# Normalising attention after the sums instead of before them, with the sums of a head pair kept together

## The chip, the cores and the metric

One core of one Trainium2 chip runs the whole kernel in one launch. Five engines work side by side, each through its own instructions in order: TensorE (PE), VectorE (DVE), ScalarE (ACT), GpSimd (POOL) and SyncE (SP), which starts the transfers. The metric is device time in microseconds (us).

## The reference

Attention over 4 batches, 12 heads, 448 positions and a head width of 64, with RMS-normalised queries and keys; then two dense blocks on the 1792x768 result, each 768 to 2048 and back.

```python
q_n, k_n = rmsnorm(q, g_q), rmsnorm(k, g_k)
scores = matmul(q_n, k_n.T) / sqrt(64)
attn = exp(scores - max(scores))
attn = attn / (sum(attn) + 1e-9)
x = matmul(attn, v)                        # then heads side by side: 1792 x 768
r = maximum(x @ w1_in, 0); x = (s * r * r + b) @ w1_out
h = x @ w2_in;             out = (h * cos(h)) @ w2_out
```

The four dense weights come in as float64 and are taken to float32 on the chip.

## The kernel before

**Attention** goes by pairs of heads, six pairs in each of four batches (24 in all). The 448 positions are four chunks of 112. A pair runs through these steps; names are those of the trace:

- `norms` (lines 115 to 146): squares of the raw queries and keys into a tile `sq` (ACT), their sums `ss` (DVE), the root by a logarithm and an exponential with a few tiny POOL instructions, then the normalised `nq` and two `nk` (POOL).
- `make_q`, `make_k`: PE turns `nq` and `nk` into PSUM tiles (`pt_q`, `pt_k`, ring `qa` of two banks); ACT and DVE split them in a high and a low part (`S`, `M0`, `M1`).
- `scores` (line 173), once per head j and chunk c, eight times a pair: two products into `sc` (PE), the negative maximum of each row (DVE, line 185), the exponential `pr` with its row sum (ACT, line 187). After each second chunk DVE adds 1e-9 to two row sums (line 191) and takes the reciprocals (line 192), and POOL multiplies the two `pr` tiles by them (line 195).
- `turn` (line 197), eight times a pair, six steps later: four PE transposes into `tp` (line 202), copied to `pT` by ACT (line 207), for the last chunk of a head by DVE (line 205). There are eleven `pT` buffers.
- `mix` (line 210), eight steps later: eight float32 products of `v` and `pT` into one bank `av`, head j=0 in its lower 64 partitions, j=1 in its upper (line 215). This text calls them the sums of a pair. Then `keep`: batches 0 and 1 are split at once into a high part `xh` (ACT) and a residue `xl` (DVE, line 92) and stay on the chip; batches 2 and 3 are copied by ACT (line 482) and written to DRAM, and come back later.

**The dense blocks** multiply with operands split in two parts, three single-pass products for one (`ph`, line 325, for the first layer of a block, `po`, lines 377 and 404, for the second). A float64 weight tile becomes float32 in `load_weight`: the transfer `raw` (two buffers), two ACT instructions (`c`, `t`), then three on DVE, the clamp of `c` (line 297), the merge of mantissa and exponent (line 300), the sign from `raw` (line 301).

**The order of the work.** The program is written as generators: attention of batch 0 alone, then the dense units of batch 0 with attention of batch 1 fed in between, and so on, by a table of debts. A planner that simulates the engines then sets the order on each engine among instructions whose inputs it takes to be there; so the eight sums of a pair need not follow each other. `follow(later, earlier)` adds a dependency by hand.

## Time and profile before

| | us |
|---|---|
| median of three runs (lowest, highest) | 1362.27 (1355.05, 1365.51) |
| the profiled execution, and its span | 1361.52, 1359.6 |
| busy: PE, DVE, ACT, POOL | 1286.0, 919.9, 819.9, 708.5 |

Matmul records carry modelled ends, so PE's busy time overlaps itself; the distance between two starts on PE says more. PE's clock was granted at 0.986 of its full speed on average. Attention's last product starts at 656 us.

### The profile page before, as it was taken

The numbers are of one execution on the slowest core, as the hardware profiler recorded it, in microseconds if no ns is written. First come the engines' busy times: TensorE is split into PE (matmuls) and PEld (weight loads), VectorE is DVE, ScalarE is ACT, GpSimd is POOL, SyncE is SP. The second block draws the span as 40 slices with busy tenths as digits, with TensorE's granted clock in tenths as the row PEclk, the third lists the DMA queues.
The fourth block names the chain that finished last, engine by engine and source line by source line (L and its number), as shares of the span: only waits on it lengthen the run. The fifth ranks groups of instructions, "written<-read, shape, count | busy, mean of one in ns | idle before, by whom it ended". The sixth has DMA issues, their size and how long they took to land.

```text
span 1359.6 us, 19381 instructions
## 1 busy us (share of the span) xinstructions
PE 1286.0 (95%) x6624; PEld 1078.5 (79%) x6624; DVE 919.9 (68%) x1641; ACT 819.9 (60%) x1826; POOL 708.5 (52%) x795
## 2 busy tenths in 40 slices
PE   4799988898999999999999999989999999999998
PEld 3455766666778787778799999879999999998997
DVE  7875999889776587554464456754566666666655
ACT  6876877777766467554334234678756666565641
POOL 5764976758666388453343232455535444453532
PEclk8899899999999999999999999999999999999999
DMA  4521435443333452111252123321111121211105
GB/s 128 156 60 41 126 118 167 123 142 103 107 103 108 129 163 64 37 44 49 84 153 79 47 76 94 93 82 47 47 47 47 47 71 49 69 40 55 47 13 162
DMA packets 84994, 116.08 MB, mean 85 GB/s; under 512 B 7584, under 2 KB 74912, under 8 KB 84896
## 3 DMA queue, kind: packets, MB, share of 16 engines
q1 hardware_dynamic: 84896, 114.85, 28.4%
q8 instruction: 52, 0.85, 0.3%
q14 instruction: 46, 0.38, 0.1%
HBM read 91.23 MB, written 23.59 MB: 84 GB/s over the span
## 4 chain that ended last, share of the span: by engine, by line
PE 57%; DVE 9%; DMA 7%; ACT 7%; issue 2%; POOL 1%; SPq 0%; DVEq 0%; ACTq 0%; POOLq 0%
PE ph L325 21%; PE po L377 13%; PE po L404 13%; PE av L215 4%; DMA raw<-in_moe_w_in_dram 4%; PE tp L202 3%; PE sc L178 3%; DMA raw<-in_moe_w_out_dram 2%; DVE gt L349 1%; DVE t L301 1%; DVE t L300 1%; DVE c L297 1%; ACT c L296 1%; DVE gt L350 1%; DMA xr<-xd 1%
## 5 line engine op out<-in xcount | busy, mean ns | idle before, releaser
L325 PE MATMUL ph<-xh,wh 128*128 128x448 f32 x768 | 281.7, 371 | 4.8 <-ACT hs L343 3.9
L325 PE MATMUL ph<-xl,wh 128*128 128x448 f32 x768 | 282.7, 370 | 0.8 <-POOL xl L92 0.7
L325 PE MATMUL ph<-xh,wl 128*128 128x448 f32 x768 | 283.0, 369 | 0.0
L355 POOL TENSOR_TENSOR gl<-gt,gh 128x448 fp32r<-128x448 f32 x128 | 155.1, 1217 | 142.3 <-ACT gh L354 142.3
L195 POOL TENSOR_SCALAR pr<-pr,r 112x448 f32<-112x448 f32 x192 | 137.3, 728 | 110.3 <-DVE r L192 68.6
L267 POOL TENSOR_TENSOR wl<-t,wh 128x384 fp32r<-128x384 f32 x144 | 154.8, 1089 | 53.0 <-ACT wh L266 50.4
L325 PEld LDWEIGHTS ph<-xh,wh 128*128 128x128 f32 x768 | 144.6, 188 | 21.4 <-ACT hs L343 4.4
L266 ACT CAST wh<-t 128x384 fp32r<-128x384 f32 x224 | 106.9, 511 | 84.4 <-PE po L377 42.6
L404 PE MATMUL po<-wh,gh 128*128 128x384 f32 x448 | 151.3, 339 | 6.1 <-DVE acc L412 5.7
L187 ACT ACTIVATE pr<-sc,small 112x448 f32<-112x448 f32 x192 | 122.1, 637 | 57.8 <-DVE small L185 56.2
L325 PEld LDWEIGHTS ph<-xl,wh 128*128 128x128 f32 x768 | 144.2, 188 | 15.3 <-POOL xl L92 1.5
L353 POOL TENSOR_TENSOR gt<-hs,gt 128x448 f32<-128x448 f32 x64 | 78.7, 1231 | 148.4 <-ACT gt L352 121.7
L325 PEld LDWEIGHTS ph<-xh,wl 128*128 128x128 f32 x768 | 144.8, 188 | 13.7 <-issue 2.8
L377 PE MATMUL po<-gh,wh 128*128 128x448 f32 x384 | 146.5, 384 | 8.7 <-DVE acc L386 7.2
L386 DVE TENSOR_TENSOR acc<-po,acc 128x448 f32<-128x448 f32 x168 | 103.1, 618 | 72.2 <-PE po L377 71.5
L404 PE MATMUL po<-wl,gh 128*128 128x384 f32 x448 | 149.4, 335 | 0.4 <-POOL wl L267 0.4
L404 PE MATMUL po<-wh,gl 128*128 128x384 f32 x448 | 149.8, 334 | 0.0
L377 PE MATMUL po<-gl,wh 128*128 128x448 f32 x384 | 142.6, 372 | 0.8 <-POOL gl L355 0.8
L377 PE MATMUL po<-gh,wl 128*128 128x448 f32 x384 | 143.1, 373 | 0.0
L185 DVE TENSOR_REDUCE small<-sc 112x1 f32<-112x448 f32 x192 | 116.7, 616 | 38.9 <-PE sc L178 37.7
L178 PE MATMUL sc<-M,S 128*112 128x448 f32 x384 | 121.9, 407 | 16.8 <-ACT pr L187 13.8
L412 DVE TENSOR_TENSOR acc<-po,acc 128x384 f32<-128x384 f32 x196 | 104.3, 550 | 43.8 <-PE po L404 43.6
(80 smaller groups left out, 2517.3 us busy)
## 6 DMA issues: line engine op xcount, KB each, us to landing
raw<-in_moe_w_in_dram SPq DMA_DIRECT2D x64, 384.0 KB, 3.5
raw<-in_moe_w_out_dram SPq DMA_DIRECT2D x64, 384.0 KB, 3.2
t<-wd SPq DMA_DIRECT2D x96, 192.0 KB, 2.4
wd<-t SPq DMA_DIRECT2D x64, 192.0 KB, 1.9
rawq<-in_q_dram SPq DMA_DIRECT2D x24, 224.0 KB, 2.8
rawk<-in_k_dram SPq DMA_DIRECT2D x24, 224.0 KB, 3.1
rawv<-in_v_dram SPq DMA_DIRECT2D x24, 224.0 KB, 3.3
xd<-xf SPq DMA_DIRECT2D x12, 224.0 KB, 2.1
```

The source lines that it names most:

```text
L178: mm = nc.tensor.matmul(sc, st[i]["S"][j][:, c * CP:(c + 1) * CP], st[i]["M"][j][n], start=(n == 0), stop=(n == 1))
L185: nc.vector.tensor_reduce(nm, sc, axis=AX.X, op=ALU.max, negate=True)
L187: nc.scalar.activation(pr, sc, AF.Exp, bias=nm, scale=1.0, accum_out=sm)
L195: nc.gpsimd.tensor_scalar(p, p, r[:, n:n + 1], 1.0, ALU.mult, ALU.mult)
L266: nc.scalar.copy(wh, w)
L267: eng.tensor_tensor(wl, w, wh.bitcast(F32), ALU.subtract)
L325: nc.tensor.matmul(h, a, m, start=(c == 0 and n == 0), stop=(c == NE - 1 and n == 2))
L355: nc.gpsimd.tensor_tensor(gl, gt, gh.bitcast(F32), ALU.subtract)
L377: marks["out"] = nc.tensor.matmul(po, a, m, start=(f == 0 and n == 0), stop=(f == CF - 1 and n == 2))
L386: nc.vector.tensor_tensor(at, po, at, ALU.add)
L404: nc.tensor.matmul(po, a, m, start=(f == 0 and n == 0), stop=(f == CF - 1 and n == 2))
L412: nc.vector.tensor_tensor(at, po, at, ALU.add)
```

## The change

- The probabilities stay unscaled: the two DVE instructions per two chunks and POOL's multiplication of each `pr` go. The eight row sums of a pair lie in one tile `sums`; after the eighth exponential POOL adds 1e-9, DVE takes eight reciprocals at once, and POOL spreads them over 64 columns each (`rb`).
- In `mix` PE transposes `rb` into a bank `rt` of the ring `qa`, ACT copies it to `x`, and after the eight sums DVE multiplies `av` by `x`. `x` lies in SBUF: batches 0 and 1 are split from there, the residue now on POOL, and batches 2 and 3 are written to DRAM from there without a further copy.
- The first product of each head in `mix` waits for the last four copies of turned tiles of the pair (`follow`).
- `pT` has ten buffers, and DVE copies three of the eight turned tiles of a pair instead of two.
- The squares of `norms` go into the tiles `nq` and the first `nk`, which the products overwrite later; `sq` is gone.
- In `load_weight` the sign is merged first, then the clamp, then mantissa and exponent.

```diff
         def norms(i):
...
-            for n, nm in enumerate("qk"):
-                sq = att.tile([CP, 8, D], F32, tag="sq", name=f"sq_{b}_{hp}_{n}", bufs=1)
-                nc.scalar.activation(sq.rearrange("p a d -> p (a d)"), st[i][nm].rearrange("p h c d -> p (h c d)"), AF.Square)
-                nc.vector.reduce_sum(ss[:, n, :], sq, axis=AX.X)
+            nq = att.tile([CP, NCH, 2, D], F32, tag="nq", name=f"nq_{b}_{hp}", bufs=1)
+            nks = [att.tile([CP, NCH, 2, D], F32, tag="nk", name=f"nk_{b}_{hp}_{j}") for j in range(2)]
+            for n, (nm, t) in enumerate((("q", nq), ("k", nks[0]))):
+                t = t.rearrange("p c h d -> p (c h d)")
+                nc.scalar.activation(t, st[i][nm].rearrange("p h c d -> p (h c d)"), AF.Square)
+                nc.vector.reduce_sum(ss[:, n, :], t.rearrange("p (a d) -> p a d", d=D), axis=AX.X)
...
         def scores(s):
...
-            if c % 2 == 0:
-                st[i]["sm"] = att.tile([CP, 4], F32, tag="small", name=f"small_{key}", bufs=3)
-            small = st[i]["sm"]
-            nm, sm = small[:, c % 2:c % 2 + 1], small[:, 2 + c % 2:3 + c % 2]
-            nc.vector.tensor_reduce(nm, sc, axis=AX.X, op=ALU.max, negate=True)
+            if s % 8 == 0:
+                st[i]["sums"] = att.tile([CP, NCH, 2], F32, tag="sums", name=f"sums_{key}", bufs=3)
+                st[i]["top"] = att.tile([CP, 8], F32, tag="top", name=f"top_{key}", bufs=3)
+            top, sums = st[i]["top"][:, s % 8:s % 8 + 1], st[i]["sums"]
+            nc.vector.tensor_reduce(top, sc, axis=AX.X, op=ALU.max, negate=True)
             pr = att.tile([CP, S], F32, tag="pr", name=f"pr_{key}", bufs=10)
-            nc.scalar.activation(pr, sc, AF.Exp, bias=nm, scale=1.0, accum_out=sm)
+            nc.scalar.activation(pr, sc, AF.Exp, bias=top, scale=1.0, accum_out=sums[:, c, j:j + 1])
             st[i]["pr", j, c] = pr
-            if c % 2:
-                r = att.tile([CP, 2], F32, tag="r", name=f"r_{key}", bufs=3)
-                nc.vector.tensor_scalar_add(r, small[:, 2:4], 1e-9)
-                nc.vector.reciprocal(r, r)
-                for n in range(2):
-                    p = st[i]["pr", j, c - 1 + n]
-                    nc.gpsimd.tensor_scalar(p, p, r[:, n:n + 1], 1.0, ALU.mult, ALU.mult)
+            if s % 8 == 7:
+                nc.gpsimd.tensor_scalar(sums, sums, 1e-9, 1.0, ALU.add, ALU.mult)
+                nc.vector.reciprocal(sums, sums)
+                rb = att.tile([CP, NCH, 2, D], F32, tag="rb", name=f"rb_{key}", bufs=1)
+                nc.gpsimd.tensor_copy(rb, sums.unsqueeze(3).to_broadcast([CP, NCH, 2, D]))
+                st[i]["rb"] = rb
...
         def turn(s):
...
-            t = att.tile([CP, S], F32, tag="pT", name=f"pT_{key}", bufs=11)
-            if kc == NCH - 1:
-                nc.vector.tensor_copy(t, tp)
+            t = att.tile([CP, S], F32, tag="pT", name=f"pT_{key}", bufs=10)
+            if kc + j >= NCH - 1:
+                done = nc.vector.tensor_copy(t, tp)
             else:
-                nc.scalar.copy(t, tp)
+                done = nc.scalar.copy(t, tp)
             st[i]["pT", j, kc] = t
+            st[i].setdefault("done", []).append(done)
...
         def mix(i):
             b, hp = pairs[i]
+            rt = ps.tile([P, 512], F32, tag="qa", name=f"rt_{b}_{hp}")[:, :S]
+            for c in range(NCH):
+                nc.tensor.transpose(rt[:, c * CP:(c + 1) * CP], st[i]["rb"][:, c, :, :].rearrange("p h d -> p (h d)"), ident[:CP, :CP])
+            x = att.tile([P, S], F32, tag="xf", name=f"xf_{b}_{hp}", bufs=1)
+            nc.scalar.copy(x, rt)
             pa = ps.tile([P, 512], F32, tag="qa", name=f"av_{b}_{hp}")[:, :S]
             for kc in range(NCH):
                 for j in range(2):
-                    nc.tensor.matmul(pa[j * D:(j + 1) * D, :], st[i]["v"][:, j, kc, :], st[i]["pT", j, kc], start=(kc == 0), stop=(kc == NCH - 1))
-            keep(b, hp, pa)
+                    mm = nc.tensor.matmul(pa[j * D:(j + 1) * D, :], st[i]["v"][:, j, kc, :], st[i]["pT", j, kc], start=(kc == 0), stop=(kc == NCH - 1))
+                    if kc == 0:
+                        for done in st[i]["done"][-4:]:
+                            follow(mm, done)
+            nc.vector.tensor_tensor(x, pa, x, ALU.mult)
+            keep(b, hp, x)
...
             nc.scalar.activation(cf, hi.bitcast(F32), AF.Copy, scale=2.0**-112)
-            nc.vector.tensor_scalar(cf, cf, VMAX, -VMAX, ALU.min, ALU.max)
             t = wp.tile([P, CW], U32, tag="t", name=f"t_{kk}", bufs=3)
             nc.scalar.activation(t, lo, AF.Copy, scale=LSCALE, bias=-0.5)
+            nc.vector.scalar_tensor_tensor(t, hi, 0x80000000, t, ALU.bitwise_and, ALU.bitwise_or)
+            nc.vector.tensor_scalar(cf, cf, VMAX, -VMAX, ALU.min, ALU.max)
             nc.vector.scalar_tensor_tensor(t, c, 3, t, ALU.logical_shift_left, ALU.bitwise_or)
-            nc.vector.scalar_tensor_tensor(t, hi, 0x80000000, t, ALU.bitwise_and, ALU.bitwise_or)
...
     def keep_on_chip(b, hp, x):
-        xs.setdefault((0, b), []).append(split(x, xa, f"1_{b}_{hp}", nc.vector))
+        xs.setdefault((0, b), []).append(split(x, xa, f"1_{b}_{hp}"))
...
     def keep_in_dram(b, hp, x):
         t = dram.tile([P, S], F32, tag=f"x_{b}_{hp}", name=f"xd_{b}_{hp}")
-        xf = pools["att"].tile([P, S], F32, tag="xf", name=f"xf_{b}_{hp}")
-        nc.scalar.copy(xf, x)
-        nc.sync.dma_start(t, xf)
+        nc.sync.dma_start(t, x)
```

What the planner makes of it is seen in the order of each engine's instructions; a name ends in batch, pair, head, chunk and a running number.

On PE, batch 1, pair 1, before: the second to fifth of the pair's sums (`av`), and the last tile turned for it (`tp`).

```order
L215 MATMUL av_1_1_2341<-pT_1_1_1_0_2162,rawv_1_1_1597 64x448
L215 MATMUL av_1_1_2341<-pT_1_1_0_1_1994,rawv_1_1_1597 64x448
L202 MATMUL tp_1_1_1_3_2242<-ident_73,pr_1_1_1_0_1882 112x112
L202 MATMUL tp_1_1_1_3_2242<-ident_73,pr_1_1_1_1_1910 112x112
L202 MATMUL tp_1_1_1_3_2242<-ident_73,pr_1_1_1_2_1969 112x112
L202 MATMUL tp_1_1_1_3_2242<-ident_73,pr_1_1_1_3_1982 112x112
L215 MATMUL av_1_1_2341<-pT_1_1_1_1_2197,rawv_1_1_1597 64x448
L215 MATMUL av_1_1_2341<-pT_1_1_0_2_2080,rawv_1_1_1597 64x448
```

The same pair in the changed kernel, from its first sum on:

```order
L387 MATMUL po_0_2_1_0_3068<-gl_0_4_0_2357,wh_0_0_1_2_0_2551 128x448
L221 MATMUL av_1_1_2220<-pT_1_1_0_0_1861,rawv_1_1_1517 64x448
L221 MATMUL av_1_1_2220<-pT_1_1_1_0_2049,rawv_1_1_1517 64x448
L221 MATMUL av_1_1_2220<-pT_1_1_0_1_1878,rawv_1_1_1517 64x448
L221 MATMUL av_1_1_2220<-pT_1_1_1_1_2079,rawv_1_1_1517 64x448
L221 MATMUL av_1_1_2220<-pT_1_1_0_2_1973,rawv_1_1_1517 64x448
L221 MATMUL av_1_1_2220<-pT_1_1_1_2_2092,rawv_1_1_1517 64x448
L221 MATMUL av_1_1_2220<-pT_1_1_0_3_2034,rawv_1_1_1517 64x448
L221 MATMUL av_1_1_2220<-pT_1_1_1_3_2123,rawv_1_1_1517 64x448
L179 MATMUL sc_1_2_1_2_2147<-M0_1_2_1_1795,S_1_2_1_1683 112x448
```

The eight products stand in a row, heads taking turns, between a dense unit and scores of the next pair. Before, four transposes stood between the third and the fourth, and the eight lay in five pieces.

On POOL, batch 0, before: scalings of the probabilities of pairs 1 and 2 and the tiny instructions of a root (`m`, `z`).

```order
L195 TENSOR_SCALAR pr_0_1_1_2_488<-pr_0_1_1_2_488,r_0_1_1_3_503 112x448
L195 TENSOR_SCALAR pr_0_1_1_3_501<-pr_0_1_1_3_501,r_0_1_1_3_503 112x448
L195 TENSOR_SCALAR pr_0_2_0_0_537<-pr_0_2_0_0_537,r_0_2_0_1_563 112x448
L195 TENSOR_SCALAR pr_0_2_0_1_561<-pr_0_2_0_1_561,r_0_2_0_1_563 112x448
L125 TENSOR_SCALAR m_1_0_1482<-ss_1_0_1475 112x16
L131 TENSOR_TENSOR z_1_0_1488<-y_1_0_1486 112x16
L132 TENSOR_TENSOR z_1_0_1488<-z_1_0_1488,m_1_0_1482 112x16
L133 TENSOR_SCALAR z_1_0_1488<-z_1_0_1488 112x16
L195 TENSOR_SCALAR pr_0_2_0_2_582<-pr_0_2_0_2_582,r_0_2_0_3_606 112x448
```

The changed kernel, batch 0, where pair 3's sums are made ready:

```order
L92 TENSOR_TENSOR xl_1_0_2_865<-xf_0_2_852,xh_1_0_2_864 128x448
L127 TENSOR_SCALAR m_1_0_1411<-ss_1_0_1403 112x16
L191 TENSOR_SCALAR sums_0_3_0_0_687<-sums_0_3_0_0_687 112x8
L133 TENSOR_TENSOR z_1_0_1417<-y_1_0_1415 112x16
L134 TENSOR_TENSOR z_1_0_1417<-z_1_0_1417,m_1_0_1411 112x16
L135 TENSOR_SCALAR z_1_0_1417<-z_1_0_1417 112x16
L194 COPY rb_0_3_1_3_838<-sums_0_3_0_0_687 112x512
L136 TENSOR_TENSOR y_1_0_1415<-y_1_0_1415,z_1_0_1417 112x16
L138 TENSOR_TENSOR nq_1_0_1404<-rawq_1_0_1399,y_1_0_1415 112x2x4x64
```

No probability passes through POOL; the sums of a pair pass once (`sums`, `rb`), and a residue `xl` stands ahead.

On ACT, batch 0, before: exponentials (`pr`) and copies of turned tiles (`pT`) of pairs 0 and 1 with weight work between (`c`, `t`, `wh`).

```order
L187 ACTIVATE pr_0_1_0_3_404,small_0_1_0_2_380<-sc_0_1_0_3_400,small_0_1_0_2_380 112x448
L296 ACTIVATE c_0_0_0_2_0_0_1356<-raw_0_0_0_2_0_0_1354 128x384
L299 ACTIVATE t_0_0_0_2_0_0_1359<-raw_0_0_0_2_0_0_1354 128x384
L266 CAST wh_0_0_0_1_0_1324<-t_0_0_0_1_0_1_1344 128x384
L207 COPY pT_0_0_1_2_430<-tp_0_0_1_2_425 112x448
L187 ACTIVATE pr_0_1_1_0_423,small_0_1_1_0_421<-sc_0_1_1_0_418,small_0_1_1_0_421 112x448
L161 CAST S_0_3_0_551<-pt_q_0_3_546 64x448
```

The changed kernel; the third `pT` row of pair 1's first head (`pT_0_1_0_2`) is the eleventh turned tile of the kernel, and so takes the buffer of the first:

```order
L309 ACTIVATE t_0_0_0_3_0_0_1314<-raw_0_0_0_3_0_0_1310 128x384
L188 ACTIVATE pr_0_1_1_3_458,sums_0_1_0_0_311<-sc_0_1_1_3_454,top_0_1_0_0_312 112x448
L207 COPY pT_0_1_0_2_509<-tp_0_1_0_2_504 112x448
L307 ACTIVATE c_0_0_0_3_0_1_1325<-raw_0_0_0_3_0_1_1323 128x384
L309 ACTIVATE t_0_0_0_3_0_1_1327<-raw_0_0_0_3_0_1_1323 128x384
L91 CAST xh_1_0_0_488<-xf_0_0_476 128x448
L207 COPY pT_0_1_1_0_548<-tp_0_1_1_0_543 112x448
L207 COPY pT_0_1_1_1_570<-tp_0_1_1_1_565 112x448
L188 ACTIVATE pr_0_2_0_0_502,sums_0_2_0_0_499<-sc_0_2_0_0_496,top_0_2_0_0_500 112x448
```

Behind that copy stand the copies of the second head and the first exponential of pair 2.

## Rows read from the trace of the kernel before

**Rows 1.** The page's busy time, share of the span and instructions of each engine.
```profile
PE 1286.0 (95%) x6624; PEld 1078.5 (79%) x6624; DVE 919.9 (68%) x1641; ACT 819.9 (60%) x1826; POOL 708.5 (52%) x795
```

**Rows 2.** Stretches: window, length, busy us (instructions) of PE, PEld, DVE, ACT, POOL; clock, DMA.
```profile
0.00:60.00 60.00, 35.52 (x160) 22.97 (x161) 49.35 (x96) 44.85 (x109) 42.94 (x66) 0.89 0.49 141
60.00:128.00 68.00, 64.11 (x336) 36.17 (x336) 45.18 (x102) 47.10 (x120) 31.83 (x55) 0.97 0.20 58
128.00:303.00 175.00, 157.25 (x802) 113.80 (x801) 159.18 (x289) 132.77 (x326) 127.03 (x159) 0.95 0.44 132
303.00:656.00 353.00, 344.13 (x1814) 263.95 (x1812) 238.56 (x446) 214.79 (x515) 211.73 (x260) 1.00 0.30 92
850.00:1360.00 510.00, 493.11 (x2575) 464.69 (x2573) 323.54 (x537) 310.74 (x615) 230.61 (x197) 1.00 0.21 61
```

**Rows 3.** Waits of PE, 0 to 128 us: waiter, releaser, us, times, longest.
```profile
PE tp L202 <- POOL pr L195: 3.7, 4, 1.7
```

**Rows 4.** Timeline of PE: start, us, engine, line, operation, tiles, records merged.
```profile
381.14 0.36 PE L325 MATMUL ph<-xh,wl 128*128 128x448 f32 x1
381.34 0.36 PE L325 MATMUL ph<-xl,wh 128*128 128x448 f32 x1
381.63 1.72 PE L215 MATMUL av<-pT,rawv 112*64 112x448 f32 x6
383.28 0.66 PE L178 MATMUL sc<-M,S 128*112 128x448 f32 x2
...
561.46 0.55 PE L202 MATMUL tp<-ident,pr 112*112 112x112 f32 x4
561.78 0.45 PE L377 MATMUL po<-gh,wh 128*128 128x448 f32 x1
...
568.61 0.97 PE L215 MATMUL av<-pT,rawv 112*64 112x448 f32 x2
569.50 0.47 PE L325 MATMUL ph<-xh,wl 128*128 128x448 f32 x1
569.81 0.36 PE L325 MATMUL ph<-xl,wh 128*128 128x448 f32 x1
```

**Rows 5.** Stretches of line 215 alone: PE busy us (records), clock, DMA.
```profile
0.00:128.00 128.00, 30.06 (x96) 0.93 0.34 97
128.00:303.00 175.00, 28.84 (x96) 0.95 0.44 132
303.00:656.00 353.00, 57.36 (x192) 1.00 0.30 92
```

**Rows 6.** Groups of DVE, 128 to 303 us: busy us, mean ns, idle before.
```profile
L300 DVE SCALAR_TENSOR_TENSOR t<-c,t 128x384 uint32<-128x384 uint32 x32 | 27.9, 875 | 0.9 <-DVE c L297 0.2
L301 DVE SCALAR_TENSOR_TENSOR t<-raw,t 128x384 uint32<-128x384 uint32 x32 | 26.0, 813 | 0.2
L191 DVE TENSOR_SCALAR r<-small 112x2 f32<-112x2 f32 x26 | 10.7, 410 | 2.2 <-ACT pr L187 2.1
L205 DVE COPY pT<-tp 112x448 f32<-112x448 f32 x12 | 7.4, 616 | 1.9 <-PE tp L202 1.8
L192 DVE RECIPROCAL r<-r 112x2 f32<-112x2 f32 x26 | 4.0, 156 | 0.2
L92 DVE TENSOR_TENSOR xl<-av,xh 128x448 fp32r<-128x448 f32 x6 | 3.7, 617 | 0.9 <-ACT xh L91 0.9
```

**Rows 7.** Groups of POOL, 128 to 303 us.
```profile
L195 POOL TENSOR_SCALAR pr<-pr,r 112x448 f32<-112x448 f32 x52 | 39.2, 766 | 14.9 <-DVE r L192 13.6 <-PE po L377 1.2
L143 POOL TENSOR_TENSOR nk<-rawk,y 112x512 f32<-112x512 f32 x15 | 17.7, 1186 | 9.9 <-PE pt_k L151 9.8
```

**Rows 8.** Two lines of DVE over the whole kernel: ns, minimum, median, maximum.
```profile
L300 DVE SCALAR_TENSOR_TENSOR t<-c,t x128: 539/557/3766, 28.6 to 1301.2; 128x384 uint32<-128x384 uint32 x128
L301 DVE SCALAR_TENSOR_TENSOR t<-raw,t x128: 530/552/2883, 30.1 to 1302.0; 128x384 uint32<-128x384 uint32 x128
```

**Rows 9.** Waits of PE, 128 to 303 us.
```profile
PE sc L178 <- ACT pr L187: 5.5, 6, 1.8
```

More of the change, by code (lines that the diff above doesn't have):

```diff
@@ L135, in norms @@
             rs = y.rearrange("p (a b) -> p a b", a=2)
-            nq = att.tile([CP, NCH, 2, D], F32, tag="nq", name=f"nq_{b}_{hp}", bufs=1)
             nc.gpsimd.tensor_tensor(
@@ L141, in norms @@
             for j in range(2):
-                nk = att.tile([CP, NCH, 2, D], F32, tag="nk", name=f"nk_{b}_{hp}_{j}")
+                nk = nks[j]
                 (nc.vector if first else nc.gpsimd).tensor_tensor(
@@ L263, in body @@
     plain = {}
+    count = {"g": 0}
     def halves(w, wh, wl, eng=nc.gpsimd):
@@ L311, in body @@
     visits = {}
-    count = {"g": 0}
     pair = []
```

## Prediction

> **What bounds the kernel now.** I read the busy shares first, then the stretches, then PE's own waits and its timeline, and last the other engines in the one stretch where PE does not decide alone. The page gives PE 95% of the span [rows 1]. The stretches split that: attention of batch 0 alone (0 to 128 us), attention of batch 1 beside the first dense units and nearly all of the first weight conversions (128 to 303), attention of batches 2 and 3 beside dense work (303 to 656), dense work alone after it [rows 2]. From 303 on PE is busy 344.1 of 353 us, so a microsecond taken from PE there is a microsecond. From 128 to 303 DVE is busy 159.2 of 175 us and PE 157.3: both have to shrink. In the first 60 us PE stands for 24.5, in the next 68 for 3.9; in both together it waits 3.7 us for POOL's scaling of the probabilities [rows 3]. Attention is over at 656, so all of the change but the order of the sign merge lies before it.
>
> The rows that matter most are PE's starts [rows 4]; the ends are modelled, so I take the distance from one start to the next. The sums of a pair (line 215) are eight float32 products; product j=0 writes the lower half of the output partitions and j=1 the upper. One product leaves two records. At 568.61 one product stands alone: the next instruction starts 0.89 us later, and I take 0.90. At 381.63 there are six records, three products, in 1.65 us. Three in less than twice the price of one means that a j=0 and a j=1 that follow each other ran side by side. So a run of sums costs 0.15 + 0.75 for each such slot of two, or for an odd one left over: one or two products 0.90, three or four 1.65, five or six 2.40, eight 3.15. Around a run there is more: the instruction before it takes 0.29 instead of 0.20 (381.34 against 381.14), and a dense or score product behind it 0.31 instead of 0.20 (569.50).
>
> **The change part by part.** The profiled execution took 1361.5 us (span 1359.6), 0.8 us under the median of the three runs, 1362.3; the sum is made against 1361.5.
>
> *Sums in one piece.* Counted in PE's order, the 192 sums stand before in 107 runs: 95 of one or two, nine of three or four, three of five. That is 95x0.90 + 9x1.65 + 3x2.40 = 107.6 us; the busy time of line 215 in the three stretches is 116.3 [rows 5], which holds a modelled tail of 0.08 a run. In the changed order there are 34 runs: seven of one or two, five of three or four, four of five or six, 18 of all eight: 6.3 + 8.3 + 9.6 + 56.7 = 80.9 us. Saved 26.7. Of the edges, 73 runs fewer at 0.09 save 6.6, and the runs with a dense or score product behind them fall from 63 to 27, at 0.10 each 3.6. Together 36.9 us; by batches 10.6, 11.1, 7.4 and 7.8, since in batches 2 and 3 the planner still breaks half of the pairs up.
>
> *The transposed reciprocals.* Four transposes per pair, at the price of a turned tile, 0.32 us (561.46 to 561.78), and up to 0.10 more behind them, as behind the sums: 24x0.4 = 9.6 us on PE. Transposes stand in more pieces than before (216 returns to single-pass products against 164), 52x0.03 = 1.6. Net of PE: 36.9 - 11.2 = 25.7, by batches about 7.8, 8.3, 4.6 and 5.0.
>
> *Scaling leaves POOL.* 192 instructions, 0.77 us each between 128 and 303 [rows 7], go; per pair come one tiny one, the spread of the reciprocals (not in the trace; nearest is the keys' product on the same 112x512, 1.19 us [rows 7], as the upper bound and nothing, if it is hidden, as the lower) and for batches 0 and 1 the residue of the output split, which leaves DVE. POOL loses some 3 us a pair and bounds nothing. The reciprocals are ready long before PE turns them: in PE's order their transposes stand eight sums and several tiles behind. I put both at nothing; if POOL were late, PE would stand at these transposes instead of at the probabilities, where it now loses 3.7.
>
> *DVE.* Per pair four additions at 0.41 and four reciprocals at 0.16 go (2.26 us), one reciprocal of eight values (0.16), one copy of a turned tile (0.62) and the product with the sums come. That product reads PSUM and SBUF; the nearest row is the output's residue at 0.62, which goes from DVE for batches 0 and 1 [rows 6]. Net 2.26 - 0.16 - 0.62 = 1.5 us a pair there, nine for the six pairs of 128 to 303, and 0.9 a pair later, where DVE decides nothing. ACT loses one copy and gains one of the same size.
>
> *Squares written into the query and key tiles, ten turned tiles instead of eleven.* No instruction more. The square now waits until PE has turned the earlier key; POOL's key product, a little later, already waited for that, 9.8 us in the middle stretch [rows 7]. Between nothing and those 9.8 us, I take nothing: the planner has put the square behind PE's transposes.
>
> *Sign first.* The raw weights come free one or two DVE instructions earlier, of 0.88 us or less [rows 6]. In the last 510 us PE stands only 17 [rows 2], so the most this can give is a few of them; I take nothing.
>
> *By stretch.* 303 to 656: 4.6 + 5.0 = 9.6, all of it on the path. 128 to 303: 8.3 on PE and nine on DVE, so 8. 0 to 128: 7.8 on PE and up to 3.7 from POOL's waits, less what the end of the stretch pays: the last pair's sums, which could start before its last turned tile was copied, now all follow it, 3.15 - 0.90 = 2.3 us. Part of PE's gain falls in the first 60 us, where PE waits for others anyway; I take 7. Sum 24.6: 1361.5 - 24.6 = 1336.9, so **1337 us**.
>
> **A rule that speaks for more.** Where POOL is busy, DVE's conversions run long: from 128 to 303 the merge of the mantissa takes 875 ns and that of the sign 813 on average [rows 6], over the whole kernel 557 and 552 in the median [rows 8]: 32x0.32 + 32x0.26 = 18.5 us lost. The Trainium skill (SBUF — State Buffer, section SBUF: two separate sides) says that VectorE and GpSimd lock one pair of ports, and that the loser stands for the whole instruction; the trace agrees in that both run long in the stretch in which POOL is busy 127 of 175 us, but names no holder. By that rule fewer POOL instructions give DVE time back, and it makes a rival below.
>
> **The rivals.**
>
> (a) *POOL was in DVE's way.* The scalings hold 39.2 of POOL's 127.0 us in the middle stretch [rows 2, 7], 31%. If DVE's 18.5 us shrink by that share, 5.7 come back, less the share of six residues and six spreads at 1.19 (14.3 of 127, 2.1): 3.6. With DVE ahead, PE's 5.5 us of waiting for the exponentials [rows 9] can go too, and some of the granted clock, 0.89, 0.97 and 0.95 up to 303 us [rows 2]: the missing 0.11x60 + 0.03x68 + 0.05x175 = 17.4 us went to stretches at 1.2 instead of 2.4 GHz, and I let a fifth to a half of it return, 4 to 9. For: DVE is busiest there. Against: other POOL work stays. 1337 less 13 to 18: about 1321.
>
> (b) *The saving is swallowed before 303.* If the first two stretches are held by the chain from scores over maximum and exponential to the turned tile, PE gets there only its removed wait of 3.7, and the end of batch 0 pays 2.3. Then 9.6 + 1.4: 1350.5. For: PE stands 46 us before 303. Against: from 60 to 128 it stands only 3.9 of 68 us, and DVE, its nearest competitor, shrinks too.
>
> (c) *ACT stands for the sums: slower.* Ten turned tiles hold one pair and two tiles of the next; with the sums in one piece the third tile of the next pair has no buffer until the first sum has run. In PE's order that sum stands behind another turned tile and a score tile: 0.32 + 0.40 + 0.09 + 0.90 = 1.7 us in which ACT's copy holds back the exponentials behind it. Were all 24 on the path, 41 us: 1337 + 41 = 1378. It decides from 24.6/24 = 1.0 us a pair. For: ACT is in order, and exponentials stand right behind that copy. Against: while it stands PE has the 3.15 us of sums to run, which cover it, and from 303 on ACT is busy 61%.
>
> (d) *The pieces do not run as counted*, or the order is spoilt by waits elsewhere: about no change, 1360.
>
> **How the numbers follow.** Forecast (gain of 16 to 34) 0.50, (a) 0.14, (b) 0.20, (c) 0.08, (d) 0.08. One per cent, 13.6 us, is about what the runs of this kernel, 1355 to 1365.5, can tell from no change. Faster by over 1%: the forecast, (a) and a third of (b), 0.70. Slower: (c) and a little of (d), 0.09. Within: 0.21. The range runs from a little below (a), 1316, for its unknown share of half-speed time, to the slow side of (b), 1357: it leaves out (c), (d) and little else.
>
> **What would show it.** Right: line 215's successor has some 84 us of busy time instead of 116, eight sums start within 3.15 us, the middle stretch ends some 15 us earlier, the last 700 us take as long as before. Wrong: new waits of PE on ACT's copies or of ACT on the sums (c); DVE's merges still over 800 ns (no (a)); PE idle before 303 as long as now (b).

## The result, and the profile after

The changed kernel takes 1349.15 us in the median against 1362.53 us before, measured beside each other; the ratio is 0.9906, with a 95% interval of 0.9888 to 0.9923. So 12.8 us are gained by the ratio and 13.4 between the medians, where 24.6 were forecast. One of the 20 executions of the changed kernel took 2052.3 us at a granted clock of 0.559, and the ratio leaves it out. The profiled execution has a span of 1348.5 us (1350.3 us in all), against 1359.6 before.

The page's busy time, to be held against [rows 1]:

```profile
PE 1268.8 (94%) x6720; PEld 1095.0 (81%) x6720; DVE 913.7 (68%) x1509; ACT 814.3 (60%) x1814; POOL 619.4 (46%) x663
```

The stretches after, cut where each batch's attention ends (columns as in [rows 2]):

```profile
0.00:60.00 60.00, 39.16 (x178) 27.68 (x178) 45.64 (x85) 44.11 (x107) 28.89 (x42) 0.85 0.56 156
60.00:123.30 63.30, 57.39 (x338) 38.55 (x336) 38.57 (x70) 42.29 (x111) 20.16 (x36) 0.93 0.14 44
123.30:297.00 173.70, 148.20 (x816) 113.89 (x817) 153.50 (x249) 131.19 (x323) 105.91 (x124) 0.96 0.45 136
297.00:646.20 349.20, 337.22 (x1870) 270.48 (x1869) 239.39 (x396) 215.38 (x518) 166.15 (x204) 0.99 0.30 91
858.00:1348.50 490.50, 476.76 (x2500) 450.87 (x2499) 319.04 (x515) 304.18 (x601) 226.53 (x192) 0.99 0.20 59
```

Cut in the same way, the kernel before has these:

```profile
0.00:128.30 128.30, 99.91 (x497) 59.20 (x497) 94.61 (x198) 92.14 (x229) 74.77 (x121) 0.93 0.34 97
128.30:302.40 174.10, 156.37 (x797) 113.24 (x798) 158.50 (x288) 132.56 (x324) 126.44 (x159) 0.95 0.44 132
302.40:656.90 354.50, 345.63 (x1821) 265.28 (x1820) 239.16 (x447) 215.59 (x517) 212.33 (x260) 1.00 0.30 91
```

| stretch | before | after | gain | forecast |
|---|---|---|---|---|
| batch 0 | 128.3 | 123.3 | 5.0 | 7 |
| batch 1 | 174.1 | 173.7 | 0.4 | 8 |
| batches 2, 3 | 354.5 | 349.2 | 5.3 | 9.6 |
| the rest | 702.7 | 702.3 | 0.4 | 0 |

In the stretch of batch 1 PE's busy time fell by 8.2 us, as forecast, and DVE's by 5.0, and yet it takes as long as before. The 5.3 us of the third row are really some three: 11 `po` products that lay in it before, about 2.3 us, are now done later. The last row came out at nothing by luck: from the first `hs` on the profiled run is 4.3 us shorter, while the stretch between attention and `hs` is 3.9 longer, 2.3 for those products and 1.7 for 3.4 us at the lower clock that the kernel before does not have there.

PE's account up to the end of attention shows where the time went. Busy time fell from 601.9 to 582.0 us (19.9 less); idle time rose from 55.0 to 64.2 (9.2 more): 10.7 in all. The granted clock cost 17.4 us before by [rows 2] and, by the rows above, 0.15x60 + 0.07x63.3 + 0.04x173.7 + 0.01x349.2 = 23.9 now. The net 25.7 us that the prediction took from PE, with 2.3 of moved products and less 6.5 of clock, make 21.5; 19.9 were seen. PE's price was about right. What failed is that it did not come off the time. The clock's part is that of one execution: its mean clock was 0.979, where the executions of this kernel have 0.983 in the median.

The sums themselves, in PE's timeline (columns as in [rows 4]):

```profile
340.86 0.36 PE L387 MATMUL po<-gl,wh 128*128 128x448 f32 x1
341.15 3.23 PE L221 MATMUL av<-pT,rawv 112*64 112x448 f32 x16
344.31 1.06 PE L179 MATMUL sc<-M,S 128*112 128x448 f32 x4
```

Sixteen records, eight sums, take 3.16 us from start to start, against the 3.15 that [rows 4] had given. There are 34 runs, 81.97 us from start to start where 80.9 were forecast.

PE's waits in 128 to 303 us, against [rows 9]:

```profile
PE tp L202 <- DVE pT L205: 5.8, 3, 2.4
PE po L387 <- DVE acc L396: 5.6, 3, 3.5
PE sc L179 <- ACT pr L188: 3.4, 4, 1.7
PE po L387 <- POOL wl L278: 2.8, 2, 2.5
```

POOL's scaling is gone from the waits of [rows 3]. In 128 to 303 us the transposes now wait for DVE's copies, which they did not before, and `po` waits longer for DVE's additions than before:

```profile
PE po L377 <- DVE acc L386: 3.1, 1, 3.1
```

DVE has less to do there, but its conversions are no shorter in sum than in [rows 6]: the sign, now first, takes 963 ns in the mean and the mantissa 794, together 56.0 us against 53.9 before.

```profile
L310 DVE SCALAR_TENSOR_TENSOR t<-raw,t 128x384 uint32<-128x384 uint32 x32 | 30.7, 963 | 1.4 <-ACT t L309 1.1
L312 DVE SCALAR_TENSOR_TENSOR t<-c,t 128x384 uint32<-128x384 uint32 x32 | 25.3, 794 | 0.3
L311 DVE TENSOR_SCALAR c<-c 128x384 f32<-128x384 f32 x32 | 17.5, 547 | 6.0 <-ACT c L307 5.8
```

### The profile page after: what moved, and what is told of

It reads as the page before. It is cut to its first block, busy times and chain, and to the rows that moved or that the text cites. A ratio compares the mean times of both kernels' runs of the same rounds, so it can differ in the third digit from the quotient of the medians.

```text
span 1348.5 us, 19191 instructions
## 1 busy us (share of the span) xinstructions
PE 1268.8 (94%) x6720; PEld 1095.0 (81%) x6720; DVE 913.7 (68%) x1509; ACT 814.3 (60%) x1814; POOL 619.4 (46%) x663
## 4 chain that ended last, share of the span: by engine, by line
PE 61%; DVE 10%; ACT 9%; DMA 5%; issue 3%; POOL 2%; SPq 0%; ACTq 0%; DVEq 0%; POOLq 0%
PE ph L335 23%; PE po L414 15%; PE po L387 14%; PE av L221 3%; DVE t L310 3%; PE sc L179 3%; DMA raw<-in_moe_w_out_dram 3%; PE tp L202 2%; DMA raw<-in_moe_w_in_dram 2%; DVE t L312 1%; ACT c L307 1%; DVE c L311 1%; DVE gt L360 1%; ACT pr L188 1%; DVE top L186 1%
## 5 line engine op out<-in xcount | busy, mean ns | idle before, releaser
L278 POOL TENSOR_TENSOR wl<-t,wh 128x384 fp32r<-128x384 f32 x144 | 161.7, 1137 | 101.4 <-ACT wh L277 90.5
L188 ACT ACTIVATE pr<-sc,top 112x448 f32<-112x448 f32 x192 | 121.8, 637 | 41.7 <-DVE top L186 40.8
L179 PE MATMUL sc<-M,S 128*112 128x448 f32 x384 | 127.0, 417 | 13.0 <-ACT pr L188 11.5
L307 ACT ACTIVATE c<-raw 128x384 f32<-128x384 f32 x128 | 71.0, 555 | 104.9 <-DMA raw<-in_moe_w_out_dram 57.3
L202 PE MATMUL tp<-ident,pr 112*112 112x112 f32 x768 | 117.8, 271 | 16.7 <-DVE pT L205 9.9
```

The source lines that it names most:

```text
L179: mm = nc.tensor.matmul(sc, st[i]["S"][j][:, c * CP:(c + 1) * CP], st[i]["M"][j][n], start=(n == 0), stop=(n == 1))
L188: nc.scalar.activation(pr, sc, AF.Exp, bias=top, scale=1.0, accum_out=sums[:, c, j:j + 1])
L202: nc.tensor.transpose(tp[:, c * CP:(c + 1) * CP], st[i]["pr", j, c][:, kc * CP:(kc + 1) * CP], ident[:CP, :CP])
L278: eng.tensor_tensor(wl, w, wh.bitcast(F32), ALU.subtract)
L307: nc.scalar.activation(cf, hi.bitcast(F32), AF.Copy, scale=2.0**-112)
```

## One stop followed through four engines

How a wait arises that no product of PE explains can be followed at 472 us. POOL's timeline, then DVE's (start, length, engine, line, operation):

```profile
472.80 1.17 POOL L138 TENSOR_TENSOR nq<-rawq,y 112x512 f32<-112x512 f32 x1
473.93 2.04 POOL L144 TENSOR_TENSOR nk<-rawk,y 112x512 f32<-112x512 f32 x2
475.92 0.93 POOL L348 TENSOR_TENSOR r<-r 128x448 f32<-128x448 f32 x1
476.82 1.32 POOL L278 TENSOR_TENSOR wl<-t,wh 128x384 fp32r<-128x384 f32 x1
```

```profile
472.98 4.28 DVE L310 SCALAR_TENSOR_TENSOR t<-raw,t 128x384 uint32<-128x384 uint32 x1
477.19 1.17 DVE L311 TENSOR_SCALAR c<-c 128x384 f32<-128x384 f32 x1
478.28 1.48 DVE L312 SCALAR_TENSOR_TENSOR t<-c,t 128x384 uint32<-128x384 uint32 x1
```

DVE's sign merge, 0.55 us when alone, takes 4.28: it begins behind POOL's `nq` and ends only when POOL has got through four products that follow each other without a gap, 0.41 us after the end of `r`. Behind it the clamp takes 1.17 us and the mantissa's merge 1.48. The wait goes on in ACT and PE; ACT's and PE's timelines:

```profile
479.80 0.51 ACT L277 CAST wh<-t 128x384 fp32r<-128x384 f32 x1 [5.32 <-DVE t L312]
480.58 0.55 ACT L307 ACTIVATE c<-raw 128x384 f32<-128x384 f32 x1 [0.27 <-DMA raw<-in_moe_w_in_dram]
481.03 0.53 ACT L346 ACTIVATE r<-ph 128x448 f32<-128x448 f32 x1
```

```profile
478.44 0.37 PE L335 MATMUL ph<-xl,wh 128*128 128x448 f32 x1
481.62 0.47 PE L387 MATMUL po<-gh,wh 128*128 128x448 f32 x1 [2.81 <-ACT r L346]
```

ACT stands 5.32 us at `wh`, because the merged weights are late, with the activation that PE needs queued behind it; PE stands 2.81. Then the granted clock falls, as the stretches before and behind show (the third figure from the end is the clock):

```profile
472.00:482.20 10.20, 7.39 (x41) 6.43 (x40) 8.50 (x7) 4.03 (x10) 8.83 (x10) 1.00 0.36 110
482.20:489.00 6.80, 6.35 (x20) 4.75 (x19) 5.82 (x10) 6.47 (x15) 4.73 (x6) 0.50 0.37 127
```

For 6.8 us PE runs at 1.2 instead of 2.4 GHz and loses another 3.4. Not every stop costs this: of the 23 stops of PE of more than 1 us in this trace, 11 are followed by such a stretch, which begins within 1.7 us of the stop's end and lasts 3.4 to 10.2 us. Up to 650 us ACT's wait at this line (`wh`) rose from 12.4 us (10 times) before to 20.3:

```profile
ACT wh L277 <- DVE t L312: 20.3, 9, 5.3
```

## The experiments

Each is measured in five rounds beside the kernel before. Ratios are to that kernel, with 95% intervals; most edits are against the changed kernel. There are two series, on what each part of the change is worth and on what sets the time before attention ends, and then combinations. An expectation names its theories by letters, and the measurement says which of them came true.

### The parts, one at a time

**The rule that holds the sums back.** The `follow` loop taken out of the changed kernel:

```diff
-                    if kc == 0:
-                        for done in st[i]["done"][-4:]:
-                            follow(mm, done)
```

> The changed kernel without the added wait of the first sums for the last four copies. PE's order then holds 44 runs of sums instead of 34, worth 94.0 us on PE by the prices of the prediction against 86.6 in the changed kernel. If every microsecond of PE counted: 7 us slower than the changed kernel, about 1356. Theory D (VectorE holds the stretch from 123 to 297 us, PE's saving there turned into waits): only the part outside that stretch counts, 5 us, about 1354. Rival (the added wait costs PE as much as it saves): no slower, 1349 or less.

Measured: 1347.31 us, 0.9900 [0.9878, 0.9921], the same as with it. The order has 44 runs instead of 34 and 7.4 us more of PE's work, and the time doesn't show it: the rival that the wait costs as much as it saves came true.

**The order of the sign alone.** The sign merged last again:

```diff
-            nc.vector.scalar_tensor_tensor(t, hi, 0x80000000, t, ALU.bitwise_and, ALU.bitwise_or)
             nc.vector.tensor_scalar(cf, cf, VMAX, -VMAX, ALU.min, ALU.max)
...
+            nc.vector.scalar_tensor_tensor(t, hi, 0x80000000, t, ALU.bitwise_and, ALU.bitwise_or)
```

> The changed kernel with the three VectorE merges of a weight in the old order (clamp, mantissa, sign). Prediction's step: worth nothing, 1348 to 1350. Rival (the raw buffers coming free earlier is what made the last 500 us 4 us shorter in the changed trace): 3 to 5 us slower, about 1353.

Measured: 1353.77 us, 0.9943 [0.9921, 0.9966]. The sign in front is worth some 4.6 us, though the intervals just touch. It shows after attention: from the first `hs` to the end the profiled runs take 494.8 us before, 490.5 with the change, 494.3 with the sign last, and PE's greatest wait there goes and comes back. In the six runs here with the sign first and the clamp once on DVE this stretch takes 490.5 to 492.2 us, in the five with the sign last 492.6 to 497.1. The 4.6 us rest on the medians: the profiled execution of this run, its fastest, has a span of 1348.1 us against 1348.5 with the change, since its part before `hs` was 4 us shorter. From 864 us on, in the kernel before, the changed one and this one:

```profile
PE po L404 <- DVE acc L412: 5.7, 8, 1.3
```
```profile
PE po L414 <- DVE acc L422: 1.5, 5, 0.4
```
```profile
PE po L414 <- DVE acc L422: 5.2, 8, 1.3
```

**The scaling kept, the sums held together.** The kernel before, with only the `follow` loop added:

```diff
...
+            st[i].setdefault("done", []).append(done)
...
+                    if kc == 0:
+                        for done in st[i]["done"][-4:]:
+                            follow(mm, done)
```

> The kernel before with the added wait alone: probabilities still scaled on GpSimd, sums of a pair together, no transposed reciprocals. PE's order holds 40 runs of sums instead of 107, worth 90.2 us against 123.5. If PE's time counts wherever it is saved: 33 us faster than before, 1330. If only outside the stretch of batch 1: 22, 1340. Rival (the sums wait for the last scaled tile, and ScalarE's copies for the sums): within 5 us of before.

Measured: 1376.5 us, 1.0107 [1.0075, 1.0139], slower, which none of the three expectations had, although the order holds 40 runs of sums and 33.3 us less of PE's work. The profiled execution, 1385.8 us, is the slowest of six; the others took 1373.5 to 1377.4. Its stretches:

```profile
0.00:135.10 135.10, 100.81 (x491) 64.18 (x491) 91.89 (x194) 90.97 (x226) 72.42 (x120) 0.85 0.32 90
135.10:310.40 175.30, 149.37 (x786) 110.88 (x787) 162.39 (x285) 131.30 (x321) 129.47 (x156) 0.95 0.45 135
310.40:671.90 361.50, 341.65 (x1826) 274.04 (x1825) 247.45 (x452) 220.10 (x523) 215.70 (x264) 0.97 0.29 88
```

The account again: the clock takes 0.15x135.1 + 0.05x175.3 + 0.03x361.5 = 39.9 us where the same rows of before give 17.7, so PE's busy time falls by 10.1 instead of 33.3; idle time goes from 55.0 to 80.1. The sum is 15 us more than before. All six executions show the clock's part, with 0.966 to 0.971 against 0.977 to 0.991 in the kernel before; the size of the idle time is that of the slowest.

**No normalising at all.** The kernel before without additions, reciprocals and scaling:

```diff
...
-                nc.vector.tensor_scalar_add(r, small[:, 2:4], 1e-9)
-                nc.vector.reciprocal(r, r)
...
-                    nc.gpsimd.tensor_scalar(p, p, r[:, n:n + 1], 1.0, ALU.mult, ALU.mult)
```

> The kernel before without additions, reciprocals and scaling, and nothing in their place (attention's result stays unnormalised); 111 runs of sums, as before. This prices the removal alone. Theory D (VectorE holds the stretch of batch 1): VectorE loses 13.6 us of small instructions there, the kernel is 8 to 14 us faster than before, 1348 to 1354, and the conversions take as long as now, near 800 ns. Rival (GpSimd was in VectorE's way): the conversions fall towards their median of 555 ns and the gain is 18 to 25 us, 1337 to 1344.

Measured: 1358.04 us, 0.9962 [0.9945, 0.9978]. Taking 192 POOL and 192 DVE instructions away, with nothing in their place, is worth 4 to 5 us, less than either theory had. The two merges of a conversion are shorter than in [rows 6] (875 and 813 ns), but far from 555, in 128 to 303 us:

```profile
L293 DVE SCALAR_TENSOR_TENSOR t<-c,t 128x384 uint32<-128x384 uint32 x32 | 24.6, 772 | 1.3 <-POOL z L131 0.2
L294 DVE SCALAR_TENSOR_TENSOR t<-raw,t 128x384 uint32<-128x384 uint32 x32 | 24.5, 769 | 0.3
```

**No normalising, and the sums held together.** The same kernel with the `follow` loop of the run with the scaling kept:

> The kernel before without its additions, reciprocals and scaling (the output is left unnormalised), as in the run without normalising that gave 1358.0 us, and now with the sums held together: each pair's first sums follow the copies of its last four turned tiles. In PE's order the runs of sums fall from 111 to 35 and their price, edges included, from 127.3 to 87.5 us, 39.8 less. Theory P (PE's price decides wherever nothing scales late): at least half of it comes back, 20 to 40 us, 1318 to 1338 us. Theory W (work taken from PE before 303 us returns as waits and as time at 1.2 GHz): 5 to 15 us, 1343 to 1353, with more than 55 us at 1.2 GHz against some 45. Theory H (holding the sums back costs by itself, as with the scaling kept, 1376.5 us): no faster than 1358.

Measured: 1348.0 us, 0.9887 [0.9860, 0.9914], inside the range of theory W. Stretches of the run without and of the run with `follow`:

```profile
0.00:132.40 132.40, 102.34 (x507) 61.21 (x508) 87.65 (x153) 93.01 (x233) 41.89 (x74) 0.92 0.33 94
132.40:297.70 165.30, 152.18 (x785) 107.71 (x784) 138.31 (x233) 130.50 (x319) 90.75 (x105) 0.97 0.47 143
297.70:653.00 355.30, 347.64 (x1814) 265.93 (x1813) 216.76 (x353) 217.98 (x517) 147.90 (x167) 0.99 0.29 89
```
```profile
0.00:118.70 118.70, 90.08 (x491) 60.34 (x491) 82.20 (x146) 89.58 (x226) 39.42 (x72) 0.93 0.36 103
118.70:290.10 171.40, 146.09 (x791) 111.44 (x792) 146.09 (x236) 131.10 (x323) 89.57 (x107) 0.96 0.46 138
290.10:637.00 346.90, 333.40 (x1822) 267.72 (x1821) 221.54 (x357) 217.66 (x521) 147.00 (x169) 0.99 0.30 91
```

PE's busy time falls by 32.6 us and its idle time rises by 16.6, from 50.8 to 67.4. In the middle stretch PE has 6.1 us less to do and the stretch takes 6.1 longer; the theory's other half, more than 55 us at 1.2 GHz, is not seen here, since the granted clock loses about 19 us in both up to there, and over the whole span 49.5 us run at that level against 45.4. Over all executions there is a little of it: the clock is 0.980 in the median against 0.983, by estimate some 4 us. The profiled executions lie at the slow end of the one kernel's times (1360.0 us) and are the fastest of the other's (1343.0), so of the 17 us between them the medians show ten.

These runs make a ladder of medians: before 1362.5; no normalising 1358.0; sums together 1348.0; the change's own normalising, squares, ten buffers and third DVE copy 1353.8 (sign last); sign first 1349.15. So normalising away 4.5, sums together 10, the change's own normalising with what came beside it -5.8, sign 4.6. The third copy alone is worth 5 us of that loss by the next run, so that little may be left for the reciprocals. The rungs are good to some 3 us each, and the run with the scaling kept shows that they don't add in any order: there the sums held together cost 14.

### What sets the time before attention ends

**Two DVE copies of turned tiles a pair instead of three:**

```diff
-            if kc + j >= NCH - 1:
+            if kc == NCH - 1:
```

> The changed kernel with VectorE copying two of a pair's eight turned tiles, as before, instead of three. The changed trace has PE waiting 10 us for these VectorE copies before 656 us. Theory D: VectorE loses 6 x 0.62 = 3.7 us of work in the stretch of batch 1, and PE's waits on it shrink: 4 to 8 us faster than the changed kernel, about 1343. Rival H (the lost part went to half-speed clock, whoever copies): unchanged, 1349. Rival A (ScalarE, which gets the copies, is late instead): 2 to 6 us slower.

Measured: 1344.03 us, 0.9859 [0.9835, 0.9882]: 5 us faster than the change as theory D had it, the intervals apart, and the fastest of the kernels here that leave nothing out. The third copy moves 24x0.61 = 14.6 us of work from ACT to DVE, and a third of that shows in the time.

**The clamp left out:**

```diff
-            nc.vector.tensor_scalar(cf, cf, VMAX, -VMAX, ALU.min, ALU.max)
```

> The changed kernel with the clamp of the converted weights left out: 128 VectorE instructions less, 32 of them, some 0.5 us each, in the stretch of batch 1. Theory D: that stretch, now 174 us, shortens by 8 us or more, PE's waits for VectorE's copies and additions there (11.4 us) at least halve, and the kernel takes 1335 to 1341. Rival (the stretch is held by the chain of one pair through all engines, or by the clock): it shortens by less than 3 us, total 1345 to 1350.

Measured: 1327.02 us, 0.9745 [0.9722, 0.9769], 22 us faster, more than theory D's 8 to 14. The stretches of batches 0, 1 and 2 with 3 shrink by 4.1, 7.2 and 8.9 us:

```profile
0.00:119.20 119.20, 92.09 (x514) 61.69 (x514) 84.53 (x143) 85.94 (x217) 45.85 (x78) 0.94 0.35 102
119.20:285.70 166.50, 145.39 (x815) 111.88 (x815) 142.47 (x217) 131.62 (x323) 109.31 (x124) 0.98 0.47 141
285.70:626.00 340.30, 333.63 (x1871) 271.42 (x1870) 221.37 (x373) 214.53 (x518) 165.42 (x204) 0.99 0.31 94
```

**The clamp done twice:**

```diff
             nc.vector.tensor_scalar(cf, cf, VMAX, -VMAX, ALU.min, ALU.max)
+            nc.vector.tensor_scalar(cf, cf, VMAX, -VMAX, ALU.min, ALU.max)
```

> The changed kernel with the clamp of the converted weights done twice on DVE (32 more instructions of 0.55 us, 17.5 us of work; the result stays the same). Leaving the clamp out had given 22 us. Theory D (DVE's work and the conversions' chain decide up to 303 us): slower by 10 to 25 us, 1359 to 1374, the middle stretch longer by 5 to 10. Theory W (leaving it out shifted the planner's order and the time at 1.2 GHz): within 6 us of 1349.

Measured: 1372.61 us, 1.0066 [1.0040, 1.0092], 23.5 us slower than the change. Taking away and doubling give about the same size with opposite signs, as theory D had it, and theory W's 6 us are excluded. Part of both passes through the clock, which up to the end of attention loses 13.7 us without the clamp, 23.9 with it and 29.0 with it twice. The stretch of batch 1 with the clamp twice:

```profile
126.50:310.60 184.10, 152.99 (x816) 116.17 (x817) 164.04 (x281) 132.77 (x323) 111.51 (x124) 0.93 0.43 128
```

PE stands 31.1 us there, 25.5 with the change, 21.1 without the clamp; its waits for DVE's copies are 7.5, 5.8 and 1.6 us. The first and the last of these:

```profile
PE tp L202 <- DVE pT L205: 7.5, 5, 3.6
```
```profile
PE tp L202 <- DVE pT L205: 1.6, 2, 0.8
```

**The clamp on POOL:**

```diff
-            nc.vector.tensor_scalar(cf, cf, VMAX, -VMAX, ALU.min, ALU.max)
+            nc.gpsimd.tensor_scalar(cf, cf, VMAX, -VMAX, ALU.min, ALU.max)
```

> The changed kernel with the clamp of the converted weights on GpSimd instead of VectorE; the whole result is computed. Leaving the clamp out made the kernel 22 us faster than the changed one. Theory D (VectorE's queue is what counts, GpSimd has room): 12 to 20 us faster than the changed kernel, 1329 to 1337. Rival (the clamp's step to GpSimd and back lengthens each conversion, and GpSimd's reads hold VectorE's): 1343 or more, VectorE's other two merges over 900 ns.

Measured: 1347.52 us, 0.9893 [0.9866, 0.9919], no gain that can be told from none, although DVE's busy time falls to 134.3 us in the stretch of batch 1. So DVE's load alone is not it: the clamp is no shorter on POOL (620 ns in the mean against 575 on DVE), and the conversion still passes through it. The rival's time came true; its sign did not, since DVE's two merges take 816 and 802 ns in that stretch and not over 900. The stretch, and ACT's wait for the merged weights in the first 650 us, the largest sum in any run here:

```profile
123.50:303.30 179.80, 156.90 (x815) 117.77 (x816) 134.31 (x216) 131.91 (x323) 120.80 (x156) 0.91 0.45 131
```

```profile
ACT wh L277 <- DVE t L312: 27.6, 16, 4.8
```

**The product with the reciprocals one step later,** behind that step's maximum on DVE:

```diff
...
-            nc.vector.tensor_tensor(x, pa, x, ALU.mult)
...
+            mult = nc.vector.tensor_tensor(x, pa, x, ALU.mult)
+            if after_top and "top" in marks:
+                follow(mult, marks["top"])
```

> The changed kernel with the multiplication by the reciprocals, and what follows it, issued one step later and behind that step's maximum on VectorE. In the changed trace VectorE stands 28.7 us in front of the 24 multiplications until the sums are done, with maxima and copies queued behind. Theory W (this wait took the gain of the first 300 us): the wait falls below 8 us and the kernel is 5 to 12 us faster than the changed one, 1337 to 1344. Rival S (VectorE had slack there): 1347 to 1351. Rival Q (the two banks of the ring are held longer and PE waits for them at the next turned queries): 1352 or more.

Measured: 1347.15 us, 0.9889 [0.9859, 0.9919]. DVE's wait ahead of the 24 products falls from 28.7 to 9.8 us and the time by 2, inside the interval, as rival S had it: this wait, new with the change, was mostly slack.

### Combinations

**Two DVE copies, no `follow`** (the edits of the first run and of the run with two copies together):

> The changed kernel with DVE copying two of eight turned tiles and without the rule that a pair's first sums follow the copies of its last four tiles. PE's order has 44 runs of sums, 94.1 us with edges, against 84.2 with the two copies alone (1344.0 us). If the added wait costs PE what shorter runs give back: 1342 to 1346; if the price of the runs decides alone: 1352 to 1356.

Measured: 1354.26 us, 0.9939 [0.9919, 0.9959]: with two copies the rule is worth 10 us, as much as the runs of sums by PE's price, while with three copies it was worth nothing. **These two and the later product:**

> The changed kernel with three edits that each gave a little or nothing: DVE copies two of eight turned tiles, the sums do not follow the copies, the product with the reciprocals is issued one step later. PE's order has 39 runs of sums, 92.4 us with edges against 86.6. If the gains add (5 + 2 + 2 us), 1340; if the copy alone counts, 1344, as with that edit alone; if PE's price of the sums decides, 1350.

Measured: 1347.66 us, 0.9893 [0.9867, 0.9919]. None of the three sums came true. Each edit also makes the planner reorder the other engines, and some of that is in every comparison; its size was not measured, and what moved these two kernels stays open.

## Why the prediction was half right

- *The price of the sums* held: 34 runs, 3.16 us for eight, 82 us in all. *The transposed reciprocals*, forecast at 9.6 us of PE, take 11.0 from start to start, 1.6 of them waits. No row gives the 0.03 us that the prediction adds for each of 52 returns to single-pass products; in the trace of before a dense product takes 0.286 us from start to start in the median behind a transpose and 0.203 behind another dense product, so the term should have been some 4.3 us and not 1.6. The rung with these transposes, the third copy and the rest cost 5.8 us of time.
- *The step that failed* is "128 to 303: 8.3 on PE and nine on DVE, so 8", and with it "all of it on the path" of the next stretch. PE and DVE shrank, and the time did not: 0.4 us instead of 8, and some 3 to 5 instead of 9.6. "A microsecond taken from PE there is a microsecond" read the share of busy time as the bound. Clamp out and clamp twice (-22 and +23.5 us) show that one DVE instruction less or more in each conversion moves the time, and the pair without normalising that half of PE's saving comes back as idle time, 16.6 of 32.6 us. That the sums, in pieces, had been work that PE did while others were late is the reading that fits; no run shows it piece by piece.
- *DVE's net* was forecast at nine us in the middle stretch and came to 5.0; the two merges, which were to stay as they were, took 2.1 us more. The third copy was counted at its 0.62 us; it is worth about 0.2 us of time a pair all the same, 5 in all.
- *Sign first*, taken at nothing, was worth some 4.6 us. The prediction had the place right, the last 510 us, and rounded it away.
- *Scaling leaves POOL*, taken at nothing apart from PE's wait of 3.7: taking it away together with DVE's additions and reciprocals gave 4.5, and no run parts the two.
- *Rival (a), POOL in DVE's way*: not shown in the changed kernel, since the conversions are as long as before, though POOL is busy 20 us less in the stretch. Without normalising the two merges do take 4.7 us less in 128 to 303, near the 5.7 that (a) gave the scalings, and the time gained no more than 4 to 5. POOL does stand in DVE's way, but with all its work. In the kernel before, 113 of the 256 merges have nothing beside them for more than 0.1 us and take 549 ns in the mean (559 at most), 31 have only scalings and take 628, 21 have only `wl` and take 943. The kind alone does not tell it: all 78 merges of more than 600 ns end 0.40 to 0.42 us after a POOL instruction has ended, and so do 76 of the 77 after the change. Of the 31 beside scalings ten are held like this; beside the other 21, of 530 to 590 ns, it is the scaling that runs long, 0.79 us or more against 0.64 in the median. So the scalings held DVE little, and in turn were held by it. Above 552 ns the merges lose 53 us before and 58 after. The Trainium skill (SBUF — State Buffer, section SBUF: two separate sides) has the loser stand for the winner's whole instruction. The trace agrees that it stands, on either side, and its merges that stood end 0.40 to 0.42 us after that instruction; at 472.98 us one stood through several instructions in a row.
- *Rival (b)*, the saving swallowed before 303, gave 1350.5, and the time is near it, but by luck, not as it was meant: batch 0 gained 5.0 and not 1.4, batch 1 nothing, and a part went after 303 as well. *Rival (c)*: the wait exists, but three times and not 24, and PE is not behind it for long: its waits for tiles that ACT copies are 4.8 us in the whole span. ACT's row:

```profile
ACT pT L207 <- PE av L221: 3.6, 3, 2.2
```

- *Rival (d)*, pieces that don't run as counted, is refuted by the timeline.
- *Squares and reciprocals*, taken at nothing: PE waits 11.0 us for POOL's `nq` in the whole span, 11.1 before, and never for the spread reciprocals.
- Not separated: how much of what the clamp is worth comes from DVE's load and how much from the chain DMA, ACT, DVE, ACT, POOL behind which ACT stands; the run with the clamp on POOL spent 34.1 us of its middle stretch at the lower clock level (17 us of time, against 7 in the changed kernel), which may have hidden a gain. ACT's wait at `wh` up to 650 us does not follow the time: 15.1 us without the clamp, 20.3 with it, 20.2 with it twice.

## What to carry to other kernels

A PE that is busy 95% may still be kept that way by filler, work that it does while others are late: before pricing PE's saving one to one, ask what PE will be waiting for at that place once the work is gone, and look for the chain through the in-order queues of the other engines. An engine that is busy 88% of a stretch and converts in steps that another engine's queue stands for can be priced by taking one small step out and by doubling it. Where a planner rebuilds the order, only parts measured in place can be added up, and those not safely.

## What was not expected of the hardware

DVE's merge of two tensors stood 4.28 us beside POOL's products that followed each other without a gap, against 0.55 us alone, and every merge of more than 600 ns before the change ended 0.40 to 0.42 us after a POOL instruction. POOL's busy time fell by 89 us over the kernel, and the merges got no faster, so POOL's load does not tell what it costs DVE. That its unbroken runs do is the reading of the longest merges, not tested by a run. And a wait can be paid twice: a stop of PE of 2.81 us was followed by 6.8 us at 1.2 GHz, as 11 of its 23 stops of more than 1 us were by 3.4 to 10.2 us, and in the run with the scaling kept and the sums together the clock alone took 22 us more than before.
